# Gated mix of windowed attention and SwiGLU on one core: another order of the first loads, w1's first product ahead of K, and a due-time shift for every planned operation

## The chip, the core and the metric

The kernel runs on one of the eight cores of a Trainium2 chip. A core has a matrix engine (PE; its weight loads are shown apart as PEld), a vector engine (DVE), a scalar engine (ACT), a general engine (POOL) and a queueing engine (SP). ACT and SP issue DMAs, and 16 DMA engines carry them. The engines run side by side and wait for each other through semaphores. The metric is the device time of one execution in microseconds: 235.54 us before, the median of three runs (235.48 to 235.83).

## The reference, cut to what matters

```python
x = A_x                                      # 1 x 2048 x 512, bfloat16
g = sigmoid((x * gate_w).sum(-1, keepdims=True))
# A: 32 heads of 16, causal window of 256
q, k, v = split(x @ wqkv)                    # wqkv 512 x 1536
p = softmax(where(mask, q @ k.T * 16**-0.5, -1e9))
a = (p @ v) @ wo                             # wo 512 x 512
# B: F = 1376
b = (silu(x @ w1) * (x @ w3)) @ w2
out = g * a + (1 - g) * b
```

## The kernel before

**Tiles.** The 2048 rows are taken as 16 tiles of 128, or as four chunks t = 0 to 3 of 512. The 32 heads are four column blocks c of 128 (eight heads each). The 1376 columns of w1 and w3 are ten blocks f of 128 and a rest of 96, which is split: 64 columns of each are handled in one joint product from wA, 32 of each (with the gate's column) in the tail product from wB (L778). x is kept turned in xT (columns of x on the partitions). Chunk 0 is loaded plainly into xs and turned on PE (L383); chunks 1 to 3 are turned by DMA (turn_x, L287, issued on L289).

**Work for a column block c.** For each chunk, K and Q (chain, L443) and V (L496, for c = 0 and 2, two blocks at once). Then score batches: 60 main batches of 8 matmuls (L551) and 16 edge batches of 32 (L601). All go through one PSUM tile, su, of four banks, which ACT empties with an exponential of 1.88 us (L555 into one of 9 Em buffers, L605 into one of 2 Ee buffers). POOL cuts the triangles out of Em (L560, L565) and of the lower half of Ee (L618), and DVE masks the rest of Ee (L624, L628). 16 groups of probabilities times V (L691, "PV" below) follow; DVE turns, divides and turns back their result into OT (L715 to L725).

**Work for a chunk of the SwiGLU part.** Each block f has a w1 product and a w3 product of four matmuls (both L841), a tanh on ACT (L851) and two DVE multiplications (L855, L861) into hT. Then w2 (L894). The output product with wo (L923) and the blend (L927) come at the end, and the last tile of rows in three parts (L950, L954). Apart from su, everything on PE uses four PSUM banks, ch.

**What sets the order.** Two things are written by hand: `opening` (L311: constants, 25 warm-up matmuls on a zeroed tile, the first loads) and then a plan. The plan (class Plan, L47) gets every operation with an engine, a duration, what it depends on and a due time; `emit` (L80) lists them engine by engine, taking of those that could start first the one with the earliest due time, and writes the instructions in that order. So the order on each engine is fixed when the program is built, and no engine passes over an instruction that waits. Due times come from some 25 numbers in K (L234). `landed` (L343) tells the plan when the first loads come. On PE an operation has a form: full (all 128 rows and columns), row (scores, 32 rows of the array each) or column (PV).

**Loads.** SP's queue takes the loads in the order of `opening`: x's first half, K's weights of blocks 0 and 1 (half on SP, half on ACT), Q's, w1's columns 0 to 255, w3's, V's, then x's chunk 1 turned in four pieces, w1 and w3 columns 256 to 767, and chunk 2 and the rest of w1 and w3 alternating (L317 to L332). The program has eight DMA semaphores for these queues and hands them out in turn, so from the ninth DMA on an issue waits until the one eight places earlier has landed. Chunk 3 is behind a gate (`late`, L360): a small POOL memset (L358) that stands in POOL's own order, and only behind it the four turned loads.

Of the kernel before, what the change touches and what calls it, by code (L numbers as in the profile page):

```python
# [8 lines left out]
ACT = mybir.ActivationFunctionType  # L9
BF16 = mybir.dt.bfloat16  # L10
# [5 lines left out]
P = 128  # L16
KB = 64
BIG = 3.0e38
SLACK = 0.04


PIPE = {"DVE": 0.105, "ACT": 0.112, "POOL": 0.045}
LAT = {"PE": 0.205}
SWITCH = 0.108

# [21 lines left out]
class Plan:  # L47
# [7 lines left out]
    def add(self, eng, dur, fn, deps=(), due=0.0, take=(), free=(), lat=None, form="full", port=False):  # L55
        if lat is None:
            lat = LAT.get(eng, 0.05)
        op = Op(eng, dur, fn, deps, due, list(take), list(free), lat, len(self.ops), form, port)
        self.ops.append(op)
        return op  # L60

# [90 lines left out]
def kernel(  # L152
# [20 lines left out]
    NDC = D // P  # L173
# [9 lines left out]
    VW = DH + 1  # L183
    HALF = (0, 1, 2, 3, 4)
    SCALE = float(DH) ** -0.5
    WARM = 25

    pp = ctx.enter_context(tc.tile_pool(name="pp", bufs=1))
    ps = ctx.enter_context(tc.tile_pool(name="ps", bufs=1, space=bass.MemoryType.PSUM))
    xT = pp.tile([P, NDC, S], BF16, name="xT")  # L190
    OT = pp.tile([P, NDC, S], BF16, name="OT")
    xs = pp.tile([P, 4, D], BF16, name="xs")
    warm = pp.tile([P, P], BF16, name="warm")
# [40 lines left out]
    K = {"T0": 3.834, "TA": 174.183, "TF0": -2.174, "TF1": 214.702, "PV": -18.741, "EDGE": -2.057, "HOLD": -5.699, "LEAD": -2.792, "QLEAD": -4.754, "V": 6.656, "O0": 12.623, "O1": 1.536, "O2": 8.341, "O3": 35.5, "FE": 0.655, "PE": 7.925, "VE": -2.0, "MK": 33.193, "UP": 8.561, "_km": 1.0, "_lo": 1.0, "LE": 0.445, "ADJ": 6.464, "SEP": -25.111, "BE": 6.303, "OE": 5.748, "END": 6.616}  # L234
# [52 lines left out]
    def turn_x(tq, c0=0, c1=NDC):  # L287
        for c in range(c0, c1):
            nc.sync.dma_start_transpose(out=xT[:, c, tq * 512:(tq + 1) * 512],  # L289
                                        in_=x2d[tq * 512:(tq + 1) * 512, c * P:(c + 1) * P])  # L290

    def load_w(dst, src, f0, f1, both=False):

        rows = src[:, f0:f1].rearrange("(c p) f -> p c f", p=P)
        for eng, c0, c1 in ((nc.sync, 0, 2), (nc.scalar, 2, 4)) if both else ((nc.sync, 0, 4),):
            eng.dma_start(out=dst[:, c0:c1, f0:f1], in_=rows[:, c0:c1, :])  # L296
# [9 lines left out]

    def warm_up(n):
        for i in range(n):
            nc.tensor.matmul(su[:, 0, 0:P], lhsT=warm[:], rhs=warm[:], start=True, stop=True)

    def opening():  # L311
        nc.vector.memset(warm[:], 0.0)
        constants()
        warm_up(WARM)

        nc.scalar.activation(out=gt[:, 0:4], in_=warm[:, 0:4], func=ACT.Tanh)
        load_x(0, 2, nc.sync)  # L317
        load_x(2, 4, nc.scalar)
        load_w(wqkv_sb, A_wqkv, D, D + 2 * P, True)
        nc.scalar.dma_start(out=gwr[:], in_=gate_w.rearrange("(c p) -> c p", p=P))  # L320
        load_w(wqkv_sb, A_wqkv, 0, 2 * P)
        load_w(w1_sb, B_w1, 0, 2 * P)
        load_w(w3_sb, B_w3, 0, 2 * P)
        load_w(wqkv_sb, A_wqkv, 2 * D, 2 * D + 2 * P)
# [255 lines left out]
    def edge_batch(c, h):  # L580
# [35 lines left out]
        def low(lo):  # L616
            e = Ee[ej.at["Ee"]][lo:lo + KB, :, :, 0, :]
            nc.gpsimd.affine_select(out=e, in_=e, pattern=[[0, 4], [0, 4], [1, KB]], compare_op=ALU.is_ge, fill=0.0,  # L618
                                    base=0, channel_multiplier=-1)
# [15 lines left out]
        x = add("ACT", 1.877, ex, [a], due, free=[(job, "su")])  # L635
        x.hold = HOLD
        if K["_lo"]:
            edge_ready[(c, h)] = [add("POOL", 1.2, lambda lo=lo: low(lo), [x], due) for lo in (0, KB)]
            edge_ready[(c, h)].append(add("DVE", 0.45 if not last else 0.6, high, [x], due - K["MK"], port=True))
# [111 lines left out]
    for dst, c0, src in ((wA, 0, w1_sb[:, :, F0:F0 + FA]), (wA, FA, w3_sb[:, :, F0:F0 + FA]),  # L751
                         (wB, 0, w1_sb[:, :, F0 + FA:F]), (wB, FB, w3_sb[:, :, F0 + FA:F])):
        def w_copy(dst=dst, c0=c0, src=src):
            nc.gpsimd.tensor_copy(out=dst[:, :, c0:c0 + src.shape[2]], in_=src)

        w_ab.append(add("POOL", 0.4, w_copy, [w13_in[3]], 22.0))

    b_ready = {}
    w2_in = []
# [4 lines left out]
    for tcb in range(NTC):  # L764
# [66 lines left out]
        for f in range(NFC):  # L831
# [4 lines left out]
            job = Job()  # L836
            up = job if joint else Job()

            def half(job, w, lo, hi, f=f, joint=joint, tcb=tcb):
                for dc in range(lo, hi):  # L840
                    nc.tensor.matmul(ch[job.at["ch"]][:],  # L841
                                     lhsT=wA[:, dc, :] if joint else w[:, dc, f * P:(f + 1) * P],
                                     rhs=xT[:, dc, tcb * 512:(tcb + 1) * 512],
                                     start=(dc == 0), stop=(dc == NDC - 1))


# [12 lines left out]
            def m2(job=job, up=up, rg=rg, ru=ru, f=f, joint=joint, tcb=tcb):  # L859
# [142 lines left out]
```

## Time and profile before

| | |
|---|---|
| median of three runs | 235.54 us |
| profiled execution | 236.38 us, of it 234.7 us from the first to the last instruction |
| granted PE clock | 1.000 over the span's mean |
| busy share | PE 96%, ACT 78%, DVE 77%, POOL 65% |
| matmuls recorded | 3590 |
| exponentials on ACT (L555 and L605) | 142.6 us busy in 76 instructions |
| moved by DMA | 11.57 MB; nearly all its busy time is in the first fifth |

The profiled execution is 0.84 us above the median. The profile gives for each engine when an instruction ran, how long the engine had been idle ahead of it and whose semaphore ended that. A PE matmul's shown end is modelled: matmuls overlap, so what one costs in a row of equal ones is the distance of their starts, and not its mean duration of 380 ns. A few matmul records are missing: line L841 has 316 matmul records to 336 weight loads.

### The profile page before, as it was taken

Reading aid. Unit: us, or ns where it says so; the run is one execution under the profiler, and the core shown is the slowest. Engines: PE = TensorE matmul, PEld = TensorE weight load, DVE = VectorE, ACT = ScalarE, POOL = GpSimd, SP = SyncE. Lnnn points to the kernel's source line nnn. Section 1 sums busy time; section 2 is a strip of 40 time slices with the busy share of each in tenths; the row PEclk is TensorE's granted clock in tenths of the full one; section 3 lists DMA queues with packets and bytes.
Section 4 is the critical chain, followed back from the end, with each engine's and each line's share of the span. In section 5 each row is a group of like instructions: output and inputs, shape, how many; then the busy total and the mean of one; then the engine's idle time right before and its main releaser. Section 6 shows DMA issues by size and latency. Waiting matters only on the chain.

```text
span 234.7 us, 8251 instructions
## 1 busy us (share of the span) xinstructions
PE 225.7 (96%) x3590; PEld 116.1 (49%) x3626; DVE 179.5 (77%) x318; ACT 182.8 (78%) x165; POOL 153.6 (65%) x245
## 2 busy tenths in 40 slices
PE   8899999999999999999999999999999999999995
PEld 7454644555454444446464556435444445445553
DVE  5455985973789897988297988969498978869675
ACT  3488998976779899887889999988778997887310
POOL 7164979579765986565668768697669855474500
PEclk9999999999999999999999999999999999999999
DMA  6999034600004000000000002200000002120102
GB/s 191 193 210 291 4 45 108 189 20 1 3 19 120 3 8 17 3 3 3 0 4 3 3 4 62 53 3 4 0 3 3 3 6 56 58 91 6 67 25 89
DMA packets 20652, 11.57 MB, mean 49 GB/s; under 512 B 10024, under 2 KB 20616, under 8 KB 20616
## 3 DMA queue, kind: packets, MB, share of 16 engines
q1 hardware_dynamic: 19920, 10.62, 18.1%
q8 instruction: 28, 0.46, 0.9%
q10 hardware_dynamic: 696, 0.43, 0.6%
q14 instruction: 8, 0.07, 0.1%
HBM read 6.85 MB, written 2.10 MB: 38 GB/s over the span
## 4 chain that ended last, share of the span: by engine, by line
PE 80%; SPq 6%; DMA 6%; POOL 4%; issue 2%; DVE 1%
PE ch L841 26%; PE ch L894 15%; PE ch L443 10%; PE ch L691 8%; PE su L551 7%; PE ch L923 6%; SPq L289 5%; PE ch L496 4%; DMA wqkv_sb<-in_A_wqkv_dram 2%; DMA w_sb<-in_B_w_dram 2%; PE su L601 2%; SPq L296 1%; DMA xT<-in_A_x_dram 1%; POOL Ee L618 1%; PE ch L950 1%
## 5 line engine op out<-in xcount | busy, mean ns | idle before, releaser
L555 ACT ACTIVATE Em<-su 128x2048 bf16<-128x2048 f32 x60 | 112.6, 1877 | 24.8 <-PE su L551 20.8
L841 PE MATMUL ch<-xT,w_sb 128*128 128x512 bf16 x301 | 76.3, 380 | 1.6 <-issue 0.8
L560 POOL TENSOR_SCALAR_AFFINE_SELECT Em<-Em 64x512 bf16<-64x512 bf16 x60 | 43.4, 724 | 36.5 <-ACT Em L555 35.6
L618 POOL TENSOR_SCALAR_AFFINE_SELECT Ee<-Ee 64x1024 bf16<-64x1024 bf16 x32 | 37.6, 1174 | 16.3 <-ACT Ee L605 15.0
L841 PEld LDWEIGHTS <-w_sb 128*128 128x128 bf16 x320 | 28.4, 98 | 34.4 <-issue 4.9
L565 POOL TENSOR_SCALAR_AFFINE_SELECT Em<-Em 64x512 bf16<-64x512 bf16 x56 | 37.3, 667 | 3.3
L855 DVE SCALAR_TENSOR_TENSOR h<-tt,ch 128x512 bf16<-128x512 bf16 (+1 forms) x44 | 29.8, 678 | 11.1 <-ACT tt L851 10.7
L894 PE MATMUL ch<-w_sb,hT 128*128 128x512 bf16 x141 | 36.1, 380 | 1.0 <-issue 0.8
L443 PE MATMUL ch<-xT,wqkv_sb 128*128 128x512 bf16 (+1 forms) x131 | 34.1, 369 | 1.8 <-DMA wqkv_sb<-in_A_wqkv_dram 0.9
L532 POOL COPY vs<-vs 64x256 bf16<-64x256 bf16 x64 | 28.9, 452 | 7.3 <-DVE vs L520 2.7
L605 ACT ACTIVATE Ee<-su 128x2048 bf16<-128x2048 f32 x16 | 30.0, 1878 | 4.2 <-PE su L601 3.1
L861 DVE SCALAR_TENSOR_TENSOR hT<-h,ch 128x512 bf16<-128x512 bf16 x40 | 27.2, 679 | 2.5 <-PE ch L841 1.0
L851 ACT ACTIVATE tt<-ch 128x512 bf16<-128x512 f32 (+1 forms) x44 | 26.2, 595 | 1.3 <-PE ch L841 1.1
L691 PEld LDWEIGHTS <-vs 128*17 128x17 bf16 x1664 | 20.6, 92 | 6.2 <-issue 4.6
L691 PE MATMUL ch<-Em,vs 128*17 128x256 bf16 (+2 forms) x672 | 22.7, 242 | 0.1
L691 PE MATMUL ch<-Ee,vs 128*17 128x64 bf16 x992 | 22.3, 193 | 0.0
L894 PEld LDWEIGHTS <-hT 128*128 128x128 bf16 x150 | 13.5, 98 | 16.2 <-issue 2.7
L898 DVE TENSOR_SCALAR bsb<-ch,omg 128x512 bf16<-128x512 f32 x15 | 11.0, 738 | 11.6 <-PE ch L894 11.4
L443 PEld LDWEIGHTS <-wqkv_sb 128*128 128x128 bf16 x136 | 12.4, 99 | 14.2 <-issue 2.1
L551 PE MATMUL su<-qT,kz 32*128 32x256 bf16 x240 | 17.3, 278 | 0.1
L496 PE MATMUL ch<-wqkv_sb,xT 128*128 128x256 bf16 x128 | 16.7, 273 | 0.2 <-DVE tn L715 0.2
L551 PE MATMUL su<-qT,k 32*128 32x256 bf16 x240 | 16.7, 268 | 0.0
(84 smaller groups left out, 245.9 us busy)
## 6 DMA issues: line engine op xcount, KB each, us to landing
out_dram<-ot SPq DMA_DIRECT2D x15, 128.0 KB, 1.7
wqkv_sb<-in_A_wqkv_dram SPq DMA_DIRECT2D x5, 256.0 KB, 4.9
w_sb<-in_B_w_dram SPq DMA_DIRECT2D x2, 608.0 KB, 5.5
w_sb<-in_B_w_dram SPq DMA_DIRECT2D x3, 384.0 KB, 3.8
w_sb<-in_B_w_dram SPq DMA_DIRECT2D x2, 512.0 KB, 5.2
w_sb<-in_B_w_dram SPq DMA_DIRECT2D x2, 256.0 KB, 6.3
wo_sb<-in_A_wo_dram SPq DMA_DIRECT2D x4, 128.0 KB, 2.3
xs<-in_A_x_dram SPq DMA_DIRECT2D x1, 256.0 KB, 2.8
```

Source lines behind the costliest of these rows:

```text
L443: nc.tensor.matmul(pst[:, t0:t1], lhsT=wqkv_sb[:, dc, col + c * P:col + (c + 1) * P], rhs=xT[:, dc, tq * 512 + t0:tq * 512 + t1], start=(d ...
L532: nc.gpsimd.tensor_copy(out=v_of(to, base, a), in_=v_of(half, 0, a))
L551: nc.tensor.matmul(su[:, s, a * 256:(a + 1) * 256], lhsT=head_keys(r, t, a), rhs=qT[r, q0:q0 + 256], start=True, stop=True)
L555: nc.scalar.activation(out=Em[job.at["Em"]][:], in_=su[:].rearrange("p s (a q) -> p s a q", a=2), func=ACT.Exp, scale=SCALE)
L560: nc.gpsimd.affine_select(out=e, in_=e, pattern=[[0, 8], [1, KB]], compare_op=ALU.is_ge, fill=0.0, base=0, channel_multiplier=-1)
L565: nc.gpsimd.affine_select(out=e, in_=e, pattern=[[0, 8], [-1, KB]], compare_op=ALU.is_ge, fill=0.0, base=-1, channel_multiplier=1)
L605: nc.scalar.activation(out=Ee[ej.at["Ee"]][:].rearrange("p s t k q -> p s (t k q)"), in_=su[:], func=ACT.Exp, scale=SCALE)
L618: nc.gpsimd.affine_select(out=e, in_=e, pattern=[[0, 4], [0, 4], [1, KB]], compare_op=ALU.is_ge, fill=0.0, base=0, channel_multiplier=-1)
L691: nc.tensor.matmul(po[32 * s:32 * s + VW, lo - 512 * w:hi - 512 * w], lhsT=vs[:, i, a * VW:(a + 1) * VW], rhs=mov, start=(n == 0), stop=(n ...
L841: nc.tensor.matmul(ch[job.at["ch"]][:], lhsT=wA[:, dc, :] if joint else w[:, dc, f * P:(f + 1) * P], rhs=xT[:, dc, tcb * 512:(tcb + 1) * 512],
L855: nc.vector.scalar_tensor_tensor(out=h1[job.at["h1"]][ru, :], in0=tt[job.at["tt"]][rg, :], scalar=1.0, in1=ch[job.at["ch"]][rg, :], op0=AL ...
L894: nc.tensor.matmul(bps[:], lhsT=ht[:, mm * P:(mm + 1) * P], rhs=w2_sb[0:fs, f, :], start=(f == 0), stop=(f == NFC - 1))
```

## The change

- **First loads.** After x, both queues take w1's columns 0 to 255 (half each), and then SP takes K's weights, w3's columns 0 to 255, Q's, V's, w1's and w3's columns 256 to 767, then x's chunk 1 turned by DMA, then w1's rest, a quarter of chunk 2, w3's rest and the other three quarters. So 1 MB of w1 and w3 stands ahead of chunk 1, which stood behind it before.
- **First product.** w1's block f = 0 for chunk 0 is done in two halves of 256 rows, as K and Q of that chunk already were, so that its first half needs only two of the four turned tiles.
- **ACT's queue.** The two ACT loads now stand ahead of the table load and of the small tanh (L316); gate_w's load stands behind them.
- **Warm-up.** 26 matmuls on the constant 1.0, in place of 25 on a tile that DVE zeroes first. The zeroing and the tile are gone.
- **The plan.** A list SHIFT adds a number of its own to the due time of each operation, by its place in the list of operations. All 25 numbers in K differ. `landed` has new times and tells the w3 loads apart. Some durations of the plan differ (POOL's overlap 0.0 in place of 0.045, L618 1.15 in place of 1.2, L624 0.6 in place of 0.45), and chunk 3's gate is due at 20.5 in place of 25.8.

```diff
-PIPE = {"DVE": 0.105, "ACT": 0.112, "POOL": 0.045}
+SHIFT = [
+    0, 0, 0, 0, 0, 0, 0, 0, 0, 0, 0, 0, 0, 0, 0, 0, 0, 0, 8.18, -2.15, 2.11, -2.04, -9.96, 0, -14.5, -9.88, 3.82,
...
+]
+PIPE = {"DVE": 0.105, "ACT": 0.112, "POOL": 0.0}
...
-        op = Op(eng, dur, fn, deps, due, list(take), list(free), lat, len(self.ops), form, port)
+        n = len(self.ops)
+        due += SHIFT[n] if n < len(SHIFT) else 0.0
+        op = Op(eng, dur, fn, deps, due, list(take), list(free), lat, n, form, port)
...
-    WARM = 25
+    WARM = 26
...
-            nc.tensor.matmul(su[:, 0, 0:P], lhsT=warm[:], rhs=warm[:], start=True, stop=True)
+            ones = nc.const_aps.tensor_like(1.0, ident[:])
+            nc.tensor.matmul(su[:, 0, 0:P], lhsT=ones, rhs=ones, start=True, stop=True)
...
-        nc.vector.memset(warm[:], 0.0)
         constants()
         warm_up(WARM)
-        nc.scalar.activation(out=gt[:, 0:4], in_=warm[:, 0:4], func=ACT.Tanh)
         load_x(0, 2, nc.sync)
         load_x(2, 4, nc.scalar)
-        load_w(wqkv_sb, A_wqkv, D, D + 2 * P, True)
+        load_w(w1_sb, B_w1, 0, 2 * P, True)
+        nc.scalar.activation(out=gt[:, 0:4], in_=nc.const_aps.tensor_like(1.0, gt[:, 0:4]), func=ACT.Tanh)
         nc.scalar.dma_start(out=gwr[:], in_=gate_w.rearrange("(c p) -> c p", p=P))
+        load_w(wqkv_sb, A_wqkv, D, D + 2 * P)
+        load_w(w3_sb, B_w3, 0, 2 * P)
         load_w(wqkv_sb, A_wqkv, 0, 2 * P)
-        load_w(w1_sb, B_w1, 0, 2 * P)
-        load_w(w3_sb, B_w3, 0, 2 * P)
         load_w(wqkv_sb, A_wqkv, 2 * D, 2 * D + 2 * P)
-        turn_x(1)
         load_w(w1_sb, B_w1, 2 * P, 6 * P)
         load_w(w3_sb, B_w3, 2 * P, 6 * P)
+        turn_x(1)
+        load_w(w1_sb, B_w1, 6 * P, F)
         turn_x(2, 0, 1)
-        load_w(w1_sb, B_w1, 6 * P, F)
+        load_w(w3_sb, B_w3, 6 * P, F)
         turn_x(2, 1, 2)
-        load_w(w3_sb, B_w3, 6 * P, F)
         turn_x(2, 2, 4)
...
-    landed = {"x": [3.75, 3.75, 4.45, 4.45, 12.2, 21.5], "w13": [7.2, 8.1, 15.4, 18.7],
-              "qkv": [5.25, 6.2, 8.8], "gw": 8.0}
+    landed = {"x": [3.6, 3.6, 4.4, 4.4, 14.5, 20.6], "w13": [5.25, 7.45, 10.8, 16.6, 12.2, 18.8],
+              "qkv": [6.5, 8.3, 9.1], "gw": 8.0}
...
-    x_in.append(late(25.8, xT[0:1, 0, 3 * 512:3 * 512 + 2], [lambda c=c: turn_x(3, c, c + 1) for c in range(NDC)], 1.27, 2.5))
+    x_in.append(late(20.5, xT[0:1, 0, 3 * 512:3 * 512 + 2], [lambda c=c: turn_x(3, c, c + 1) for c in range(NDC)], 1.27, 2.5))
...
-            win3 = [w13_in[1]] if f < 2 else []
-            a = plan.pieces(HALF, 0.2155, lambda lo, hi, half=half, job=job: half(job, w1_sb, lo, hi),
-                            xt_ready[tcb] + win + last_up + (w_ab if joint else []), due, [(job, "ch")])
+            win3 = [w13_in[1 if f < 2 else 4 if f < 6 else 5]]
+            if tcb or f:
+                a = plan.pieces(HALF, 0.2155, lambda lo, hi, half=half, job=job: half(job, w1_sb, lo, hi),
+                                xt_ready[tcb] + win + last_up + (w_ab if joint else []), due, [(job, "ch")])
+            else:
+                a = add("PE", 0.436, lambda half=half, job=job: half(job, w1_sb, 0, NDC, 0, 256),
+                        xt_ready[0][0:2] + win, due, take=[(job, "ch")])
+                a = add("PE", 0.436, lambda half=half, job=job: half(job, w1_sb, 0, NDC, 256, 512),
+                        [a] + xt_ready[0][2:4], due)
```

More of the change, by code (lines that the diff above doesn't have):

```diff
@@ L192 @@
     xs = pp.tile([P, 4, D], BF16, name="xs")
-    warm = pp.tile([P, P], BF16, name="warm")
     wqkv_sb = pp.tile([P, NDC, 3 * D], BF16, name="wqkv_sb")
@@ L232 @@
     ch = [ps.tile([P, 512], F32, name=f"ch_{i}") for i in range(4)]
-    K = {"T0": 3.834, "TA": 174.183, "TF0": -2.174, "TF1": 214.702, "PV": -18.741, "EDGE": -2.057, "HOLD": -5.699, "LEAD": -2.792, "QLEAD": -4.754, "V": 6.656, "O0": 12.623, "O1": 1.536, "O2": 8.341, "O3": 35.5, "FE": 0.655, "PE": 7.925, "VE": -2.0, "MK": 33.193, "UP": 8.561, "_km": 1.0, "_lo": 1.0, "LE": 0.445, "ADJ": 6.464, "SEP": -25.111, "BE": 6.303, "OE": 5.748, "END": 6.616}
+    K = {"T0": 5.297, "TA": 206.41, "TF0": 1.484, "TF1": 225.404, "PV": -11.652, "EDGE": -4.017, "HOLD": -7.362, "LEAD": -3.173, "QLEAD": -5.466, "V": 9.67, "O0": 15.202, "O1": -11.15, "O2": 0.879, "O3": 11.614, "FE": 1.961, "PE": 21.917, "VE": -6.72, "MK": 72.039, "UP": 9.552, "_km": 1.0, "_lo": 1.0, "LE": -4.354, "ADJ": 22.279, "SEP": -69.261, "BE": 7.567, "OE": -0.078, "END": 5.97}
     plan = Plan({"su": 1, "ch": 4, "Em": len(Em), "Ee": len(Ee), "tt": 2, "h1": 2,
@@ L637, in edge_batch @@
         if K["_lo"]:
-            edge_ready[(c, h)] = [add("POOL", 1.2, lambda lo=lo: low(lo), [x], due) for lo in (0, KB)]
-            edge_ready[(c, h)].append(add("DVE", 0.45 if not last else 0.6, high, [x], due - K["MK"], port=True))
+            edge_ready[(c, h)] = [add("POOL", 1.15, lambda lo=lo: low(lo), [x], due) for lo in (0, KB)]
+            edge_ready[(c, h)].append(add("DVE", 0.6, high, [x], due - K["MK"], port=True))
         else:
@@ L754, in w_copy @@
             nc.gpsimd.tensor_copy(out=dst[:, :, c0:c0 + src.shape[2]], in_=src)
-        w_ab.append(add("POOL", 0.4, w_copy, [w13_in[3]], 22.0))
+        w_ab.append(add("POOL", 0.4, w_copy, [w13_in[5]], 22.0))
     b_ready = {}
@@ L837, with half @@
             up = job if joint else Job()
-            def half(job, w, lo, hi, f=f, joint=joint, tcb=tcb):
+            def half(job, w, lo, hi, t0=0, t1=512, f=f, joint=joint, tcb=tcb):
                 for dc in range(lo, hi):
-                    nc.tensor.matmul(ch[job.at["ch"]][:],
+                    nc.tensor.matmul(ch[job.at["ch"]][:, t0:t1],
                                      lhsT=wA[:, dc, :] if joint else w[:, dc, f * P:(f + 1) * P],
-                                     rhs=xT[:, dc, tcb * 512:(tcb + 1) * 512],
+                                     rhs=xT[:, dc, tcb * 512 + t0:tcb * 512 + t1],
                                      start=(dc == 0), stop=(dc == NDC - 1))
```

88 rows, old and new, of the table SHIFT are left out of this document.

## The prediction

> **What bounds the kernel now.** I read the page from the top: the span, the busy shares, the slices and the chain that ended last.
>
> ```profile
> span 234.7 us, 8251 instructions
> PE 225.7 (96%) x3590; PEld 116.1 (49%) x3626; DVE 179.5 (77%) x318; ACT 182.8 (78%) x165; POOL 153.6 (65%) x245
> ...
> PE   8899999999999999999999999999999999999995
> ...
> PE 80%; SPq 6%; DMA 6%; POOL 4%; issue 2%; DVE 1%
> ```
>
> PE is busy for nine tenths or more of every slice but the first two and the last, and four fifths of the chain lie on it; what is left of the chain is queueing, loads and POOL. So I asked for PE's time after 38.6 us (the first row: the stretch, its length, busy time and instructions of PE, PEld, DVE, ACT and POOL, granted clock, DMA share, GB/s) and for what PE waited there (who waited for whom: in total, times, longest).
>
> ```profile
> 38.60:232.00 193.40, 189.96 (x3182) 94.98 (x3212) 154.41 (x269) 153.56 (x133) 127.99 (x188) 1.00 0.10 29
> ...
> PE ch L894 <- issue: 0.8, 5, 0.2
> ...
> PE ch L443 <- DMA xT<-in_A_x_dram: 0.4, 1, 0.4
> ```
>
> After 38.6 us PE is idle for 3.4 of 193.4 us, in pieces of at most 0.2 us without a releaser (places where one matmul record is missing) and one of 0.4 us for x, which is the end of the wait at 38.6 itself. In that stretch no engine holds PE up. A new order can win there only by giving PE less to do; it can lose as much as it likes. What can be won by waiting less lies ahead of 38.6 us. The timeline of PE and the chain in that part:
>
> ```profile
> 1.07 2.85 PE L309 MATMUL su<-warm 128*128 128x128 bf16 x25 [1.07 <-DVE warm L312]
> 3.71 1.91 PE L383 MATMUL ch<-ident,xs 128*128 128x128 bf16 x16
> 5.63 1.22 PE L443 MATMUL ch<-xT,wqkv_sb 128*128 128x256 bf16 x8
> 7.73 1.05 PE L443 MATMUL ch<-xT,wqkv_sb 128*128 128x256 bf16 x8 [0.88 <-DMA wqkv_sb<-in_A_wqkv_dram]
> ...
> 17.70 0.38 PE L443 MATMUL ch<-xT,wqkv_sb 128*128 128x512 bf16 x1
> 18.20 0.60 PE L841 MATMUL ch<-xT,w_sb 128*128 128x512 bf16 x2
> ...
> 37.45 0.81 PE L443 MATMUL ch<-xT,wqkv_sb 128*128 128x512 bf16 x3
> 38.62 0.38 PE L443 MATMUL ch<-xT,wqkv_sb 128*128 128x512 bf16 x1 [0.36 <-DMA xT<-in_A_x_dram]
> ```
>
> ```profile
> 1.83 5.85 DMA wqkv_sb<-in_A_wqkv_dram
> 7.70 1.16 SPq L289
> ...
> 8.90 1.26 SPq L289
> ...
> 10.21 1.26 SPq L289
> ...
> 14.87 0.58 SPq L296
> ...
> 31.43 0.10 POOL xT L358
> ...
> 5.23 0.59 ACT L390 COPY xT<-ch 128x512 bf16<-128x512 bf16 x1 [2.92 <-PE ch L383]
> 11.51 2.03 SPq L296 DMA_DIRECT2D w_sb<-in_B_w_dram  x2
> 19.19 0.65 POOL L565 TENSOR_SCALAR_AFFINE_SELECT Em<-Em 64x512 bf16<-64x512 bf16 x1
> ```
>
> Three waits are to be seen: 0.88 us for Q's weights (issued at 1.83, landed 7.68), one for w3's second load at 18.2, one for x's chunk 3 at 38.6, whose loads stood behind a POOL memset that came only at 31.43.
>
> **What a matmul and a change of form cost.** Starts, not durations, count.
>
> ```profile
> 89.08 2.55 PE L841 MATMUL ch<-xT,w_sb 128*128 128x512 bf16 x11
> 91.56 0.29 PE L551 MATMUL su<-qT,kz 32*128 32x256 bf16 x4
> 91.67 0.28 PE L551 MATMUL su<-qT,k 32*128 32x256 bf16 x4
> 91.89 0.39 PE L841 MATMUL ch<-xT,w_sb 128*128 128x512 bf16 x1
> ```
>
> Eleven matmuls of 512 columns: (2.55 - 0.38) / 10 = 0.217 us each, so 0.108 for 256 columns. They end streaming at 91.46; the score batch starts 0.10 later, and the next full matmul comes at 91.89. A batch thus takes 0.43 us, of which each of its two changes of form is about 0.1.
>
> **The change part by part.**
>
> *Steady order (SHIFT, K).* In the built order both kernels have the same 60 main and 16 edge batches, the same PV matmuls and the same columns streamed; the four extra w1 matmuls are halves (8 x 0.108 for 4 x 0.217), so nothing. PE changes form 170 times before and 172 times after: PV groups stand directly beside a score batch 15 times before and 13 times after. 2 x 0.1 = **+0.2 us**, on the path. By the columns between them, two successive score batches are at least 2.49 us apart before and 2.58 after, so su is not asked for sooner. No gain here.
>
> *Chunk 3's gate.* The wait: 37.45 + 3 x 0.217 = 38.10, and PE went on at 38.62, **-0.52**. In the new POOL order the memset stands right behind the cuts of the third main batch; in the trace these ended at 19.19 + 0.65 = 19.84, and with the first copies to wA and wB ahead of it I put it at 22 to 25. The same 7.2 us from memset to landing (31.43 to 38.6) give 32 at the latest; the first use, V of chunk 3, comes after some 36 us of PE's order. Nothing is late next there.
>
> *w1's and w3's second loads.* The wait: 17.70 + 0.22 = 17.92 to 18.20, **-0.28**. Their issue moves from 11.51 on to about 4.4 and 5.3 us (behind V's; the second waits by the ring of eight semaphores for w1's ACT half). An issue takes SP about 0.6 us (14.87). Even 7 us from issue to landing serves their first use, at about 15.5 and 18.5.
>
> *w1 first, then K.* w1 takes K's place in the queues and K takes Q's. w1's product fills 5.63 to 6.85 as K's did, and K then waits until 7.68 as Q did: **0**. Bounds: -0.9 if K's load lands before 6.85, since K's own loads had landed when PE took them up at 5.63; +0.2, as the third and fourth tile of x are turned 0.2 later behind the two warm-up matmuls that now stand between them. I take 0, the row that is the same place of the same queue.
>
> *Warm-up and ACT's queue.* Warm-up may begin some 0.1 us earlier and has one matmul more; PE begins to turn x when x lands at 3.71 either way: 0. ACT's two issues come 0.2 us earlier than behind the tanh, but the sixteen turns run from 3.71 without a gap, so x's second half is not waited for: 0, at best -0.2 by w1's half. The tanh and table load, now behind, are covered by ACT's idle time until 5.23 us. The gate column's matmul is beside a change of form in both: 0 (bounds -0.2 and +0.1).
>
> *Chunk 1 behind 1 MB.* This is what the change pays with, and its price is the open one. Before, its last piece was issued at 10.21 and landed 3.9 us later, at 14.1:
>
> ```profile
> xT<-in_A_x_dram SPq DMA_TRANSPOSE x1, 3.9
> ...
> 14.50:17.50 3.00, 2.95 (x21) 1.18 (x21) 1.54 (x3) 2.33 (x3) 2.53 (x6) 1.00 1.04 335
> ```
>
> Now w3's second load is issued until about 5.9; the first piece took SP from 4.93 to the next at 7.70, 2.8 us, and each further one 1.3, so the last is issued at 5.9 + 2.8 + 2.6 = 11.3 and lands at 15.2 if only SP matters. If instead all 1 MB passes ahead of it at the 335 GB/s of that window, it lands 1048 / 335 = 3.1 us later than before, at 17.2. Needed: from K's start at 7.73 the built order has, before Q of chunk 1, 8 halves each for K and Q and 16 matmuls of 256 columns for V, 14 of 512 for w1 and w3 and 3 for K of the next block, two score batches and the gate column (about 0.2): 32 x 0.108 + 17 x 0.217 + 2 x 0.43 + 0.2 = 8.2, so 15.9. The wait is between 0 and 17.2 - 15.9 = 1.3; I take 0, since SP's pace, and not the bytes, set these landings in the trace.
>
> The Trainium skill, page "DMA: Bandwidth & Descriptors", section "Queues, rings and completion order", says that a queue's descriptors are consumed in ring order on each DMA engine, and that SP has one such row. By that rule the turned pieces cannot overtake w1 and w3, whatever SP's pace, and the sum would carry the later landing. The trace agrees as far as it goes:
>
> ```profile
> 3.67 0.66 SPq L296 DMA_DIRECT2D wqkv_sb<-in_A_wqkv_dram  x1
> 4.93 6.54 SPq L289 DMA_TRANSPOSE xT<-in_A_x_dram  x4
> ...
> wqkv_sb<-in_A_wqkv_dram SPq DMA_DIRECT2D x1, 256.0 KB, 6.4
> ...
> xT<-in_A_x_dram SPq DMA_TRANSPOSE x1, 5.7
> ```
>
> V's load (issued 3.67) landed 6.4 us later, at 10.0, and the first turned piece, issued at 4.93 right behind it, at 10.6.
>
> **Sum.** +0.2 - 0.52 - 0.28 = **-0.6 us**. The profiled execution took 236.38 us, so 235.8 there; it stands 0.84 above the median, and by the same difference the median comes to 235.54 - 0.6 = **234.9 us**. The start alone moves this between -1.7 (K's load early, gate column free) and +0.3.
>
> **The rivals.**
>
> *K's load lands early.* Then PE does not wait at 7.7. For it: K's own loads were there when PE began at 5.63. Against it: the load in that very place took 5.85 us. Time: 234.9 - 0.9 = 234.0.
>
> *Chunk 1 comes late.* Ring order and 1 MB ahead; the landing at 17.2 against a need at 15.9 costs 1.3: 234.9 + 1.3 = 236.2. Up to a wait of 0.1 it is still faster, between 0.1 and 1.1 no change, beyond that slower. Against it: between 8 and 10 us DMA moved little (the last number of this row, in GB/s), so there is room for much of the 1 MB to pass unseen.
>
> ```profile
> 8.00:10.00 2.00, 1.95 (x14) 1.12 (x13) 0.47 (x2) 1.27 (x3) 0.00 (x0) 1.00 1.41 97
> ```
>
> *The edge masks come late (slower).* PV needs both POOL cuts of the edge batch. The path at the end of the trace:
>
> ```profile
> 214.63 0.38 PE L601 MATMUL su<-qT,kz 32*128 32x64 bf16 x28
> 215.23 1.86 ACT L605 ACTIVATE Ee<-su 128x2048 bf16<-128x2048 f32 x1
> 217.15 2.37 POOL L618 TENSOR_SCALAR_AFFINE_SELECT Ee<-Ee 64x1024 bf16<-64x1024 bf16 x2 [1.37 <-ACT Ee L605]
> ...
> L560 POOL TENSOR_SCALAR_AFFINE_SELECT Em<-Em 64x512 bf16<-64x512 bf16 x60 | 43.4, 724 | 36.5 <-ACT Em L555 35.6
> ```
>
> From 214.63 to 219.52 are 4.9 us with POOL free. By the columns between them, PV stands 5.4 to 5.65 us behind its last edge batch six times in the new order, and once before (5.62); elsewhere it is 6 us or more. If POOL still has a pair of cuts to do (2 x 0.7) when the exponential ends, PV comes 0.7 to 0.9 us late. One such group leaves the gain at nothing, two make the kernel slower: 234.9 + 1.6 = 236.5. For it: nothing in the trace before shows these distances in number, and PE's share leaves no room elsewhere. Against it: the one group at 5.62 did not wait.
>
> *The change does not do what it says.* PE does the same work, and the start is one wait for one other load; if chunk 3's wait comes back somewhere else, 235.5. I count it into the second rival's middle.
>
> **How the numbers follow.** Forecast 0.48 (own range 234.5 to 235.3), K early 0.09, chunk 1 late 0.19 (235.2 to 236.2), edge masks late 0.24. A measurement of this kernel tells about 0.2% (0.47 us) from no change. Faster: K early 0.09 and three quarters of the forecast, 0.36, make 0.45. Same: 0.12 of the forecast and half of the second rival, 0.10, make 0.22. Slower: the rest of the second rival and the third, 0.33. The range goes from K early (233.8) to the third rival (236.5).
>
> **What would show it.** In the new profile: PE's wait ahead of K's first matmul, near 0.9 us and ended by K's load; no wait for x ahead of chunk 3's first product; no wait for w1 or w3 after 12 us; Q of chunk 1 without a wait for x at about 16 us; and after 38 us again no idle time of PE but the short pieces without a releaser. Wrong would be: an idle of PE ended by x near 16 us (second rival), or idle ahead of L691's new line ended by POOL's cuts of Ee (third); and any difference in busy PE time above 0.3 us.

## The result, and the profile after

The changed kernel takes 236.84 us (median of four runs, 236.49 to 237.07) against 235.62 for the kernel before in the same comparison: a ratio of 1.0055, with a 95% interval of 1.0034 to 1.0077. It is slower by 1.2 us where the prediction had it 0.6 faster, and outside its range. The profiled execution took 236.49 us, 0.35 below the median; that of the kernel before had been 0.84 above its own. So the two profiles, nearly equal in time, hide the difference, and the stages have to be compared one by one.

The page of the changed kernel: the span, the busy shares, PE's slices and the chain.

```profile
span 234.8 us, 8252 instructions
PE 224.5 (96%) x3590; PEld 116.4 (50%) x3631; DVE 183.4 (78%) x317; ACT 181.9 (77%) x165; POOL 153.1 (65%) x245
...
PE   7999999999998999999999999999999999999995
...
PE 83%; DVE 6%; issue 5%; ACT 5%; DMA 1%; ACTq 0%
```

SP's queue (6%), DMA (6%) and POOL (4%) have left the chain almost wholly; DVE and ACT, of which there was 1% or nothing, have come in with 11%. (PE's busy time is 1.2 us lower than before; 41 matmul records are missing against 36, by the number of weight loads, and five of 0.217 us make 1.1 of it.) The start, by PE's timeline:

```profile
4.12 1.03 PE L476 MATMUL ch<-ident,xs 128*128 128x128 bf16 x8 [0.33 <-DMA xs<-in_A_x_dram]
...
5.78 1.29 PE L934 MATMUL ch<-xT,w_sb 128*128 128x256 bf16 x8
6.91 1.04 PE L536 MATMUL ch<-xT,wqkv_sb 128*128 128x256 bf16 x8
...
14.94 1.03 PE L536 MATMUL ch<-xT,wqkv_sb 128*128 128x512 bf16 x4
...
17.53 1.04 PE L934 MATMUL ch<-xT,w_sb 128*128 128x512 bf16 x4
18.41 0.38 PE L536 MATMUL ch<-xT,wqkv_sb 128*128 128x512 bf16 x1
18.62 1.03 PE L934 MATMUL ch<-xT,w_sb 128*128 128x512 bf16 x4
```

PE turns x from 4.12 us on (3.71 before), goes from w1's product to K's without waiting, and waits neither for chunk 1 (14.94) nor for w1's and w3's second loads (17.5 to 19). Chunk 3's memset now stands at 21.38 us, its data are there at 28.8, and PE uses them at 36 without a wait. The waits that were to be saved ahead of 40 us are gone, though x comes 0.4 us later. The larger loss lies behind. Where PE waited from 38 to 232 us (who for whom; total, times, longest):

```profile
PE ch L536 <- DVE hT L954: 1.0, 1, 1.0
...
PE ch L784 <- DVE hT L954: 0.3, 1, 0.3
PE su L694 <- ACT Em L648: 0.3, 1, 0.3
PE ch L934 <- DVE h L948: 0.2, 1, 0.2
PE ch L934 <- DVE hT L954: 0.2, 1, 0.2
```

Apart from one wait of 0.3 us for ACT's exponential, and the short pieces without a releaser (left out here), it is DVE's SwiGLU work that PE waits for. The place of the longest one, by the timelines of DVE, POOL and PE:

```profile
70.22 0.69 DVE L948 SCALAR_TENSOR_TENSOR h<-tt,ch 128x512 bf16<-128x512 bf16 x1 [0.91 <-ACT tt L944]
70.83 0.66 DVE L717 TENSOR_TENSOR Ee<-Ee,medge 128x512 bf16<-128x512 bf16 x1
71.41 1.36 DVE L721 TENSOR_TENSOR Ee<-Ee,mlast 128x512 bf16<-128x512 bf16 x1
72.69 0.68 DVE L954 SCALAR_TENSOR_TENSOR hT<-h,ch 128x512 bf16<-128x512 bf16 x1
...
70.06 1.15 POOL L711 TENSOR_SCALAR_AFFINE_SELECT Ee<-Ee 64x1024 bf16<-64x1024 bf16 x1
...
71.31 1.18 POOL L711 TENSOR_SCALAR_AFFINE_SELECT Ee<-Ee 64x1024 bf16<-64x1024 bf16 x1
...
70.93 1.46 PE L934 MATMUL ch<-xT,w_sb 128*128 128x512 bf16 x6
73.42 0.59 PE L536 MATMUL ch<-xT,wqkv_sb 128*128 128x512 bf16 x2 [1.03 <-DVE hT L954]
```

The two masks of an edge batch (L717, L721) hold DVE from 70.83 to 72.77 us; hT comes that much later, its PSUM bank is freed later, and K's next product, which needs the bank, starts at 73.42 instead of 72.4. Neither mask is shown as waiting: they count as busy. What they wait for can be read from POOL's rows. L717 began while POOL's first cut ran, and ended 0.28 us after it (70.06 + 1.15 = 71.21, against 71.49). L721 began 0.10 us after POOL's second cut had begun and ended at 72.77, 0.28 us after that cut (71.31 + 1.18 = 72.49). The same at 97 us, where the mask has 1024 columns (the row of POOL joins two cuts, from 95.51 to 97.87):

```profile
96.75 1.66 DVE L717 TENSOR_TENSOR Ee<-Ee,medge 128x1024 bf16<-128x1024 bf16 x1
...
95.51 2.36 POOL L711 TENSOR_SCALAR_AFFINE_SELECT Ee<-Ee 64x1024 bf16<-64x1024 bf16 x2 [1.55 <-ACT Ee L698]
...
38.65 0.68 DVE L717 TENSOR_TENSOR Ee<-Ee,medge 128x1024 bf16<-128x1024 bf16 x1
...
37.50 2.84 POOL L711 TENSOR_SCALAR_AFFINE_SELECT Ee<-Ee 64x1024 bf16<-64x1024 bf16 x2
```

There the mask ended at 98.41, 0.54 us after the cut. At 38.65 it was ahead of the second cut by a hair, took 0.68 us, and the pair of cuts is 0.48 longer: now POOL waited. Over all its masks of 1024 columns the changed kernel needs 950 ns each, the kernel before 850:

```profile
L717 DVE TENSOR_TENSOR Ee<-Ee,medge 128x1024 bf16<-128x1024 bf16 x12 | 11.4, 950 | 0.1
...
L624 DVE TENSOR_TENSOR Ee<-Ee,medge 128x1024 bf16<-128x1024 bf16 x12 | 10.2, 850 | 0.0
...
180.65 1.36 DVE L624 TENSOR_TENSOR Ee<-Ee,medge 128x1024 bf16<-128x1024 bf16 x1
```

So the kernel before meets POOL too (the last row is its longest mask), but PE waits nowhere in it for h or hT. A lengthened mask costs time only where PE's next operand or bank comes late by it.

The Trainium skill, page "SBUF — State Buffer", section "SBUF: two separate sides", says that VectorE and GpSimd have one pair of ports in common, which is an exclusive lock: for a VectorE instruction with two inputs in SBUF (as these masks) against a GpSimd instruction that reads SBUF (as the cuts), whoever starts first has it for its whole instruction, and the other blocks. These rows agree: what POOL still had to do when the masks began was 1.08 and 1.12 us, and the masks took 0.95 and 0.98 longer than a free one (0.41 in a row below, 0.68). The prediction did not draw on that rule.

Why more of it now: in the plan of the kernel before, all 16 masks stand behind both cuts of their edge batch. In the new plan 10 of the 16 stand ahead of one cut (8) or of both (2). Which number of the plan does this can be counted by computing the plan again, without a run. It is not MK, by which a mask's due time is drawn forward: with the old 33.2 in place of 72.0 the new order stays the same, operation for operation. Without SHIFT 12 masks still stand ahead of a cut. It is POOL's overlap: set to 0.0 instead of 0.045 in the kernel before, with nothing else changed, it puts 11 of the 16 masks ahead of a cut. `emit` takes what can start first, and lets a mask start 0.045 us before a cut's planned end; with an overlap of 0.045 POOL's next cut ties with the mask and is taken, with 0.0 the mask is earlier. No run has this one number changed alone.

The plan itself (`port`) never lets a mask and a cut overlap by more than these 0.045 us: it has the mask at 70.5 and the cut behind it at 71.1. But on the chip no semaphore orders the two, and POOL was there first.

### The profile page after: what moved, and what is told of

It reads as the page before. It is cut to its first block, busy times and chain, and to the rows that moved or that the text cites. A ratio compares the mean times of both kernels' runs of the same rounds, so it can differ in the third digit from the quotient of the medians.

```text
span 234.8 us, 8252 instructions
## 1 busy us (share of the span) xinstructions
PE 224.5 (96%) x3590; PEld 116.4 (50%) x3631; DVE 183.4 (78%) x317; ACT 181.9 (77%) x165; POOL 153.1 (65%) x245
## 4 chain that ended last, share of the span: by engine, by line
PE 83%; DVE 6%; issue 5%; ACT 5%; DMA 1%; ACTq 0%
PE ch L934 24%; PE ch L993 15%; PE ch L536 10%; PE ch L784 9%; PE su L644 8%; PE ch L1022 6%; PE ch L589 6%; PE su L694 2%; DVE h L948 2%; ACT Em L648 2%; DMA xs<-in_A_x_dram 1%; DVE hT L954 1%; ACT Ee L698 1%; PE ch L1049 1%; ACT tt L944 1%
## 5 line engine op out<-in xcount | busy, mean ns | idle before, releaser
L934 PE MATMUL ch<-xT,w_sb 128*128 128x512 bf16 (+1 forms) x304 | 76.9, 377 | 2.5 <-issue 1.4
L653 POOL TENSOR_SCALAR_AFFINE_SELECT Em<-Em 64x512 bf16<-64x512 bf16 x60 | 40.7, 678 | 22.0 <-ACT Em L648 19.9
L658 POOL TENSOR_SCALAR_AFFINE_SELECT Em<-Em 64x512 bf16<-64x512 bf16 x56 | 38.7, 692 | 24.7 <-ACT Em L648 23.1
L711 POOL TENSOR_SCALAR_AFFINE_SELECT Ee<-Ee 64x1024 bf16<-64x1024 bf16 x32 | 39.2, 1226 | 16.5 <-ACT Ee L698 15.4
L934 PEld LDWEIGHTS <-w_sb 128*128 128x128 bf16 x324 | 29.0, 98 | 34.6 <-issue 6.0
L993 PE MATMUL ch<-w_sb,hT 128*128 128x512 bf16 x140 | 35.4, 380 | 0.9 <-issue 0.6
L536 PE MATMUL ch<-xT,wqkv_sb 128*128 128x512 bf16 (+1 forms) x127 | 33.6, 366 | 2.0 <-DVE hT L954 1.0
L625 POOL COPY vs<-vs 64x256 bf16<-64x256 bf16 x64 | 28.3, 442 | 3.9 <-DVE vs L599 0.8
L993 PEld LDWEIGHTS <-hT 128*128 128x128 bf16 x150 | 13.4, 98 | 15.7 <-issue 1.7
L644 PEld LDWEIGHTS <-kz 32*128 32x128 bf16 x240 | 6.0, 91 | 21.9 <-issue 20.6
```

The source lines that it names most:

```text
L536: nc.tensor.matmul(pst[:, t0:t1], lhsT=wqkv_sb[:, dc, col + c * P:col + (c + 1) * P], rhs=xT[:, dc, tq * 512 + t0:tq * 512 + t1], start=(d ...
L644: nc.tensor.matmul(su[:, s, a * 256:(a + 1) * 256], lhsT=head_keys(r, t, a), rhs=qT[r, q0:q0 + 256], start=True, stop=True)
L653: nc.gpsimd.affine_select(out=e, in_=e, pattern=[[0, 8], [1, KB]], compare_op=ALU.is_ge, fill=0.0, base=0, channel_multiplier=-1)
L658: nc.gpsimd.affine_select(out=e, in_=e, pattern=[[0, 8], [-1, KB]], compare_op=ALU.is_ge, fill=0.0, base=-1, channel_multiplier=1)
L934: nc.tensor.matmul(ch[job.at["ch"]][:, t0:t1], lhsT=wA[:, dc, :] if joint else w[:, dc, f * P:(f + 1) * P], rhs=xT[:, dc, tcb * 512 + t0:t ...
L993: nc.tensor.matmul(bps[:], lhsT=ht[:, mm * P:(mm + 1) * P], rhs=w2_sb[0:fs, f, :], start=(f == 0), stop=(f == NFC - 1))
```

## The experiments

The kernel before was run again beside each group of runs; its median there was between 235.36 and 235.95 us. So ratios may be compared across groups, and times only to within some 0.6 us.

### Is it the mask, or what it waits for?

The changed kernel again, with a second profile (no edit).

> The changed kernel, unchanged, with a second profile beside the same runs of the kernel before. Theory: the wait at 72 us is not a chance of one execution, since POOL's second cut and VectorE's mask start in the same order each time: PE is again idle for 0.9 to 1.1 us ahead of the product at 73.4 us, and the time is 1.004 to 1.007 of the kernel before. Rival: the order of the two is a toss-up, 0.1 us apart; then this profile may show no wait there.

236.98 us, 1.0048 of the kernel before (1.0024 to 1.0073). The wait is there again, with the same numbers:

```profile
71.24 1.36 DVE L721 TENSOR_TENSOR Ee<-Ee,mlast 128x512 bf16<-128x512 bf16 x1
...
73.25 0.59 PE L536 MATMUL ch<-xT,wqkv_sb 128*128 128x512 bf16 x2 [1.04 <-DVE hT L954]
```

It belongs to the order, not to one execution. Next, the pair of masks moved behind hT:

```diff
+        high = [e for e in order if e[1].fn.__name__ == "high"]
+        for k, n in ((3, 1),):
+            dve = [e for e in order if e[1].eng == "DVE"]
+            to = dve[dve.index(high[k]) + n]
+            order.remove(high[k])
+            order.insert(order.index(to) + 1, high[k])
         self.order = order
```

> The changed kernel with one pair of VectorE masks (L717 and L721 at 70.8 us) put behind the hT multiplication that followed it; nothing else differs. Theory: in the changed kernel this pair held VectorE until 72.7 us and with it a PSUM bank, and cost PE 1.03 us; moved, PE's idle time at 72.4 to 73.4 us shrinks to 0.3 us or less and the kernel comes out 0.8 to 1.1 us faster than the changed one: 235.8 to 236.0 us, 1.001 to 1.002 of the kernel before. Rival: PE is only late at the next place (the copies of K behind the pair are then 0.6 us later); the time stays within 0.3 us of 236.84, 1.004 or more.

236.61 us, 1.0033 (1.0013 to 1.0053): by its time the rival (0.23 us below the changed kernel), by its ratio between the two. The wait at 72 us is gone, and PE waits at the next place instead, since the pair still takes 1.9 us:

```profile
71.89 1.11 DVE L723 TENSOR_TENSOR Ee<-Ee,medge 128x512 bf16<-128x512 bf16 x1
72.92 0.87 DVE L727 TENSOR_TENSOR Ee<-Ee,mlast 128x512 bf16<-128x512 bf16 x1
...
75.23 0.21 PE L790 MATMUL ch<-Em,vs 128*17 128x64 bf16 x4 [1.06 <-ACT k L565]
```

So the place of the mask is not the cause by itself. Next, what it waits for is taken away: POOL's second cut. This kernel leaves one block of probabilities uncut and serves for its time alone.

```diff
-            edge_ready[(c, h)] = [add("POOL", 1.15, lambda lo=lo: low(lo), [x], due) for lo in (0, KB)]
+            edge_ready[(c, h)] = [add("POOL", 1.15, lambda lo=lo: None if last and lo and c == 0 else low(lo), [x], due)
+                                  for lo in (0, KB)]
```

> The changed kernel without one of its 64 x 1024 cuts on POOL (the one that ran from 71.31 to 72.49 us; its part of the output is then wrong). Theory: a VectorE mask that starts while a POOL instruction runs stands until that has ended (in the changed kernel a mask of 512 columns that found POOL busy lasted 0.27 us beyond the end of POOL's instruction, one of 1024 columns 0.54, whatever the length of the wait). So L721 takes 0.41 us instead of 1.36, hT starts 0.95 us sooner, PE's idle time of 1.03 us there falls to 0.1, and the time is 0.9 to 1.0 us below 236.84: 235.9 us, 1.0013 of the kernel before. Rival: the mask is slow or late by itself (its place, its operand); then L721 still takes 1 us or more and the time stays within 0.3 us.

235.59 us, 0.9997 (0.9979 to 1.0015): 1.25 us below the changed kernel, a little more than expected, and the mask at its old place takes what was expected of it.

```profile
71.19 0.41 DVE L721 TENSOR_TENSOR Ee<-Ee,mlast 128x512 bf16<-128x512 bf16 x1
71.53 0.68 DVE L955 SCALAR_TENSOR_TENSOR hT<-h,ch 128x512 bf16<-128x512 bf16 x1
...
72.26 0.59 PE L536 MATMUL ch<-xT,wqkv_sb 128*128 128x512 bf16 x2
```

One POOL instruction of 1.18 us, for whose result PE did not wait, cost as much as the whole difference. Then the same with the whole output: POOL is made to keep the plan's order by a copy of two elements that DVE has masked.

```diff
             e = Ee[ej.at["Ee"]][lo:lo + KB, :, :, 0, :]
+            if lo and (c, h) in ((0, 3),):
+                nc.gpsimd.tensor_copy(out=scrap[:], in_=Ee[ej.at["Ee"]][0:1, 0:4:3, 3, 1, 0])
...
+            if (c, h) in ((0, 3),):
+                pairs.append((edge_ready[(c, h)][1], edge_ready[(c, h)][2]))
...
+        for cut, mask in self.pairs:
+            i, j = order.index(at[cut.seq]), order.index(at[mask.seq])
+            if i < j:
+                order.insert(i, order.pop(j))
         self.order = order
```

> The changed kernel, whole output: only at the place at 71.3 us POOL's second cut waits until VectorE's masks are through (a copy of two elements of the masked tile on POOL ahead of it). Theory: nothing is wrong with the order of the masks, only with POOL's cut taking the way into SBUF 0.1 us ahead of L721; so this does what leaving the cut out did: L721 0.41 us, PE's idle time before the next product 0.1 to 0.3 us instead of 1.03, and 235.6 to 235.9 us, 0.9995 to 1.001 of the kernel before. Rival: the cut, now some 0.3 us later, and the next cuts behind it make the PV group behind it late by as much as is won; 1.004 or more.

236.02 us, 1.0009 (0.9989 to 1.0030): 0.8 us won by the times, 0.1 short of what was expected (the ratio is within it), and less than without the cut (235.59), which now comes 0.9 us later.

```profile
71.47 0.41 DVE L730 TENSOR_TENSOR Ee<-Ee,mlast 128x512 bf16<-128x512 bf16 x1
...
71.94 0.17 POOL L719 COPY scrap<-Ee 1x2 bf16<-1x2 bf16 x1 [0.64 <-DVE Ee L730]
72.19 1.16 POOL L720 TENSOR_SCALAR_AFFINE_SELECT Ee<-Ee 64x1024 bf16<-64x1024 bf16 x1
...
72.53 0.59 PE L543 MATMUL ch<-xT,wqkv_sb 128*128 128x512 bf16 x2
```

The same copy at four places:

```diff
-            if lo and (c, h) in ((0, 3),):
+            if lo and (c, h) in ((0, 3), (1, 1), (3, 0), (3, 1)):
...
-            if (c, h) in ((0, 3),):
+            if (c, h) in ((0, 3), (1, 1), (3, 0), (3, 1)):
```

> The same at four places: the pairs of cuts at 70.1, 95.5, 184.2 and 185.7 us of the changed kernel. Theory: the other places where PE is late (0.28 us at 98.8, 0.37 at 187.5) are of the same kind, masks of 1.66, 1.59 and 1.03 us against 0.68 when POOL is idle; so another 0.4 to 0.6 us beside the single place: 235.0 to 235.4 us, 0.997 to 0.9985 of the kernel before. Rival: there the cuts themselves are waited for (PV needs both); then nothing is won beside the single place, or PE is late for POOL instead.

235.36 us, 0.9985 (0.9971 to 1.0000), within what was expected. The mask at 96.2 us takes 0.68 us instead of 1.66, and the answer on PE's waits between 38 and 232 us is empty. Undoing this one fault is worth 236.84 - 235.36 = 1.5 us by the times, and 1.6 by the ratios (0.0070 of 235.6).

```profile
96.20 0.68 DVE L726 TENSOR_TENSOR Ee<-Ee,medge 128x1024 bf16<-128x1024 bf16 x1
96.86 0.69 DVE L965 SCALAR_TENSOR_TENSOR hT<-h,ch 128x512 bf16<-128x512 bf16 x1
97.93 0.69 DVE L582 CAST qT<-ch 128x512 bf16<-128x512 f32 x1 [0.39 <-PE ch L543]
```

### Which of the saved waits were there to be saved?

The kernel before, unchanged, twice more.

> The kernel before, unchanged, with a second profile. Theory: the 0.88 us wait for Q's weights at 7.7 us in the first profile was one late load (it landed at 7.68 though 14 of its 16 DMA engines were done by 6.18) and not the rule; now Q's load lands by 6.9, PE waits at most 0.2 us there, and the profiled execution takes 235.5 to 235.8 us. Rival: the wait belongs to the place of the queue, as the prediction had it; then Q's load lands at 7.5 or later again and PE waits 0.7 us or more. Time against the kernel before: 1.000 by both.

> The kernel before, unchanged, a third profile. Theory: the waits for loads differ from one execution to the next: Q's at 6.7 us between 0 and 0.9, chunk 3's at 37 to 39 us between 0 and 0.6, w3's at 17 near 0.3 each time. Rival: the first profile was the exception, and this one shows no wait at chunk 3, as the second. Time: 1.000 by both.

Ratios 0.9986 (0.9962 to 1.0010) and 0.9993 (0.9971 to 1.0015), as it must be. PE's waits from 4 to 232 us, first in the second profile, then in the third:

```profile
PE ch L443 <- DMA wqkv_sb<-in_A_wqkv_dram: 0.4, 1, 0.4
```

```profile
PE ch L443 <- DMA xT<-in_A_x_dram: 0.7, 1, 0.7
```

Q's load landed at 7.68, 6.65 and 5.97 us in the three profiles, and the wait for it was 0.88, 0.37 (between theory and rival) and 0; chunk 3 cost 0.36, 0 and 0.68 of idle time. The wait for w3's second load is too short for this view, yet PE is idle for 0.28 us there each time, and goes on 0.05 us after the load has landed. So Q's place in the queue is not what made it late. Chunk 3's gate alone, moved in the kernel before:

```diff
+        gate = next(e for e in order if e[1].eng == "POOL" and e[1].due == 25.8)
+        turns = [e for e in order if e[1].eng == "SP"][:4]
+        far = [e for e in order if e[1].fn.__name__ in ("near", "far")][5]
+        for e in [gate] + turns:
+            order.remove(e)
+        i = order.index(far) + 1
+        order[i:i] = [gate] + turns
         self.order = order
```

> The kernel before with one part of the change alone: chunk 3's gate and its four loads behind the sixth cut on POOL (some 20 us) instead of at 30 us. The prediction took -0.52 us from the one profile it had. Theory now: that wait belonged to an execution whose loads all came late; in the second profile chunk 3 had landed when it was asked for; so nothing is won: within 0.15 us of the kernel before, 0.9994 to 1.0006. Rival: the prediction's term, 0.9978.

234.98 us against 235.95, 0.9953 (0.9926 to 0.9980). My theory fell, and the prediction's term stands: this is worth 0.5 us or more, and by the median nearly twice the term (0.97). To see whether the landing really decides, the gate two cuts later than it was:

```diff
+        pool = [e for e in order if e[1].eng == "POOL"]
+        to = pool[pool.index(gate) + 2]
...
+        i = order.index(to) + 1
+        order[i:i] = [gate] + turns
```

> The kernel before with chunk 3's gate two cuts on POOL later (1.4 us). The early gate alone made the kernel before 0.47% faster though a second profile of it showed no wait at chunk 3. Theory: in ordinary executions chunk 3 lands within some tenths of a us of its use at 38 us, sometimes ahead and sometimes behind, so that PE waits 0 to 1 us, 0.5 or more on average; then 1.4 us more of delay costs all of it beyond: 1.0 to 1.4 us, 1.004 to 1.006, and the profile shows PE waiting 1.0 us or more for x at 37 to 40 us. Rival: chunk 3 usually lands with room, and the early gate gained in another way; then less than 0.5 us, 1.002 or less.

236.27 us against 235.36, 1.0026 (1.0005 to 1.0048), between theory and rival; the profile has the wait:

```profile
37.88 0.38 PE L451 MATMUL ch<-xT,wqkv_sb 128*128 128x512 bf16 x1 [0.95 <-DMA xT<-in_A_x_dram]
```

So in ordinary executions chunk 3 lands at about its use, sometimes behind it. Then the second loads of w1 and w3 ahead of chunk 1, together with the early gate, in the kernel before:

```diff
-        turn_x(1)
         load_w(w1_sb, B_w1, 2 * P, 6 * P)
         load_w(w3_sb, B_w3, 2 * P, 6 * P)
+        turn_x(1)
```

> The kernel before, with only two parts of the change: the second loads of w1 and w3 ahead of chunk 1, and chunk 3's gate behind the sixth cut on POOL. The prediction put them at -0.28 and -0.52 us. Theory now: the second profile of the kernel before shows the wait for w3 (0.28) and none for chunk 3, so the compared runs gain 0.2 to 0.3 us in all: 0.9987 to 0.9992 of the kernel before. Rival: the prediction's sum, -0.8 us: 0.9966. Third: chunk 1 behind 1 MB is late in the order of before, whose PE asks for it 2 us sooner (at 13.0 us): slower, 1.003 or more.

236.04 us, 1.0019 (1.0004 to 1.0035): slower, as in the third case, but by less than its 1.003. That is 1.1 us more than with the gate alone by the times, 1.6 by the ratios (0.0066 of 235.8). Chunk 1's pieces land at 12.9 to 15.7 us, where they had landed at 9.6 to 13.2 with the gate alone, and the old order asks for them at 13.25:

```profile
13.25 0.38 PE L450 MATMUL ch<-xT,wqkv_sb 128*128 128x512 bf16 x1
14.82 1.35 PE L450 MATMUL ch<-xT,wqkv_sb 128*128 128x512 bf16 x3 [1.19 <-DMA xT<-in_A_x_dram]
```

The prediction's second rival thus comes true for the old order, with a wait of 1.19 us. The Trainium skill's rule on ring order (page "DMA: Bandwidth & Descriptors", section "Queues, rings and completion order") agrees with it: the first piece landed at 12.9 us, behind w3's load at 12.4. But the run does not show the rule by itself, for of the 3.3 us by which that piece came later, 2.1 are a later issue on SP (7.00 us against 4.87). The changed kernel does not pay this because its own order asks for chunk 1 only at 14.94.

### The later x

In the changed kernel x's first half lands at 4.07 us instead of 3.65. The tanh first on ACT again:

```diff
+        ones = nc.const_aps.tensor_like(1.0, gt[:, 0:4])
+        nc.scalar.activation(out=gt[:, 0:4], in_=ones, func=ACT.Tanh)
         load_x(0, 2, nc.sync)
         load_x(2, 4, nc.scalar)
         load_w(w1_sb, B_w1, 0, 2 * P, True)
-        nc.scalar.activation(out=gt[:, 0:4], in_=nc.const_aps.tensor_like(1.0, gt[:, 0:4]), func=ACT.Tanh)
```

> The changed kernel with ACT's warming tanh (and its table load) ahead of ACT's loads of x and w1, as before the change. Theory: the two halves of x, issued at the same moment on two queues, share the DMA engines, and the first half lands 0.4 us later (4.07 against 3.65 us); with the tanh first it lands at 3.65 again, PE starts turning at 3.7 and the kernel is 0.3 to 0.4 us faster than the changed one: 236.45 us, 1.0037. Rival: x's first half lands at 4.0 or later all the same, or what follows (w1's half, the third and fourth tile of x) is later by as much: within 0.15 us of the changed kernel.

236.65 us, 1.0046 (1.0029 to 1.0063): 0.2 us below the changed kernel, between theory and rival. x still landed at 4.02, as the rival has it: ACT's issue came only 0.07 us later (0.88). With the tanh on DVE's zeroed tile, as before the change, ACT issues at 1.05:

```diff
-        ones = nc.const_aps.tensor_like(1.0, gt[:, 0:4])
-        nc.scalar.activation(out=gt[:, 0:4], in_=ones, func=ACT.Tanh)
+        nc.vector.memset(warm[:], 0.0)
+        nc.scalar.activation(out=gt[:, 0:4], in_=warm[:, 0:4], func=ACT.Tanh)
```

> The changed kernel with the tanh first on ACT and on the VectorE memset as before the change, so that ACT issues its half of x at 1.05 us again, 0.2 us behind SP's. Theory: the two halves share the DMA engines, and that 0.2 us is what let the first half land at 3.65 to 3.70 us; now it does so again and PE turns from 3.75 on; but K's load, third in its queue, still lands at 6.4 to 6.7 us, so that PE waits there and the kernel gains 0.1 to 0.2 us at most over the changed one: 1.0045 to 1.005 of the kernel before. Rival: all of the 0.3 us is won, 1.0040 or less. Third: x lands at 4.0 us again, so the issue time has nothing to do with it.

```profile
3.80 1.03 PE L478 MATMUL ch<-ident,xs 128*128 128x128 bf16 x8
...
6.73 1.26 PE L538 MATMUL ch<-xT,wqkv_sb 128*128 128x256 bf16 x9 [0.19 <-DMA wqkv_sb<-in_A_wqkv_dram]
```

x lands at 3.75 again, and K's load, third in its queue, is waited for instead; 236.84 us, 1.0059 (1.0037 to 1.0080). Nothing is won, where 0.1 to 0.2 us was expected: what the later x costs, the third load costs otherwise.

### Together

The four waiting cuts, x early, and two matmuls of w1's second block (w, w2) drawn ahead of K (k) to fill that wait, where two of K's next block (k1, k2) take their old place:

```diff
+        k, k1, w = (next(e for e in order if e[1].seq == n) for n in (46, 245, 813))
...
+        k2, w2, w3 = (next(e for e in order if e[1].seq == n) for n in (246, 814, 815))
+        for e in (k1, k2, w, w2):
+            order.remove(e)
+        i = order.index(w3)
+        order[i:i] = [k1, k2]
+        order.insert(order.index(k), w)
+        order.insert(order.index(k), w2)
```

> The changed kernel with the cuts that wait at four places, ACT's tanh first (x's first half at 3.7 us), and, since PE then waits 0.36 us for K's load, two matmuls of w1's second column block drawn ahead of K, with two of K's next block put where they stood. Theory: the start is bound by the third load, and these 0.43 us of work fit ahead of it; so 0.3 us less than with the cuts alone (235.36): 235.0 us, 0.997 of the kernel before. Rival: the next loads (w3 at 7.5, Q at 8.4 us) take over and PE waits there: 0.9985 as with the cuts alone.

235.35 us against 235.95, 0.9972 (0.9953 to 0.9992). It beats both kernels, and its profile shows no wait for a load. But by its time (235.36 with the waiting cuts alone) the start gave nothing more, and by the ratio 0.3 us, which lies within the intervals. The best median of all is the kernel before with the early gate, 234.98 us.

## Why the prediction was wrong

- **Chunk 3's gate, -0.52.** Right. The wait is gone, nothing is late next, and the early gate alone gives 0.97 us (interval 0.5 to 1.7), so the term may have been too small.
- **Second loads of w1 and w3, -0.28.** Right: no wait at 17 to 19 us. (No run shows what this saves by itself.)
- **Chunk 1 behind 1 MB, 0.** Right for this order (the waits for it in its profiles and those of its variants are 0 to 0.2 us); with the old order of PE it costs 1.1 to 1.6, the rival's price.
- **w1 first, then K: "K then waits until 7.68 as Q did".** Wrong in the mechanism, small in the sum. K landed at 6.44. The row it was taken from showed one slow load of one execution. With that went the level: that profile, with waits of 0.88 and 0.36 us, is 0.84 above the median, while the two later ones, with 0.37 and 0.68, are within 0.2 of theirs. So a wait of 0.88 was no property of the queue.
- **Warm-up and ACT's queue, "0, at best -0.2".** Wrong: two halves issued together made the first one 0.4 us late. The wait for K that would have followed is what went instead, so the sum hardly moved.
- **Steady order: "+0.2 ... No gain here".** This is the step that failed. The two more changes of form were priced (no run shows them alone), and for DVE only the words "it can lose as much as it likes" were left. What it lost is 1.5 us: masks planned ahead of POOL's cuts that found POOL at work. The third rival saw lateness of the edge batch, and came near the time (236.5) by chance, for it had POOL's cuts late for PV; PV never waited for them. It was the cuts that held up DVE, and with it SwiGLU's work and its PSUM banks.

The sum was -0.6 and the result +1.2. Of the 1.8 between them, 1.5 is the masks. The other 0.3 is not settled, and it is more if the gate gives the 0.97 us that it gave alone: the kernel before varies by itself, from 234.45 to 237.98 us over the 113 runs made beside the experiments.

One sum of the prediction is mixed up: "-1.7 ... and +0.3" for the start sets a total beside a change. By its own bounds (K -0.9 to +0.2, gate column -0.2 to +0.1) the total would go from -1.7 to -0.3. The forecast does not rest on it.

## What to carry to other kernels

A new order of instructions is to be read for VectorE and GpSimd instructions that exclude each other, as the masks and cuts do here: where the new order has a mask between two POOL instructions, price it at the whole of the second one (1.18 us here), and look at whose buffer stands behind it. An order that only a plan assumes is no order; if it matters, one tiny instruction that reads the other's result makes it one. A planner's constant can change such an order by itself: here 0.045 us of assumed overlap decided whether masks were put between cuts. And a wait for a load seen in one profiled execution is a sample: set it against the profile's distance from the median before it becomes a term.

## What was not expected of the hardware

- A mask that starts while POOL has more than some 0.14 us left lasts until POOL's instruction has ended and 0.27 us (512 columns) or 0.52 to 0.54 us (1024) beyond, in all fifteen traces; with less left it takes its free 0.41 or 0.68 us. (In one case the two began within 0.03 us of each other, and POOL waited.) It is shown as busy all the while, so the view of waits names DVE and never POOL.
- Two loads of equal size issued at 0.82 and 0.81 us on two queues landed at 4.07 and 4.43 (in seven profiles, with 0.81 to 0.88, at 4.0 to 4.2 and 4.4 to 4.5); issued at 0.82 and 1.05, at 3.4 to 3.8 and 4.2 to 4.6, also in seven. A lead of 0.23 us brings the first 0.2 us or more and costs the second next to nothing.
- The same load in the same place of the queue landed 1.7 us apart from one execution to another (Q's, 5.97 to 7.68).
